# Attention and experts on one core: six small moves in the opening, the attention and the first slot

## The chip, the cores and the metric

The kernel runs on one NeuronCore of a Trainium2 chip. The metric is device time in microseconds (us), the median of three runs. Engines: TensorE (PE; its weight loads are PEld), VectorE (DVE), ScalarE (ACT), GpSimd (POOL) and SyncE (SP, which here issues DMAs). Each engine works through its own queue in order; semaphores tie the queues together.

## The reference

Three layers, one after the other. Attention: batch 4, 8 heads, 576 positions, head size 64, a causal window of 128 with a linear bias by distance:

```python
scores = scale * np.matmul(q, k.transpose(0, 1, 3, 2))
mask = (rel >= 0) & (rel < window)
scores = np.where(mask, scores + bias[None], -1000000000.0)
attn = np.exp(scores - scores.max(-1)); attn = attn / (attn.sum(-1) + 1e-09)
out = np.matmul(attn, v)
```

Its output (2304 tokens of 512) goes through a mixture of 8 experts of which each token uses one, `gate * (relu(x @ w1[e]) @ w2[e])` with the expert chosen by the largest gating logit, and then through a dense layer, `(relu(x @ w_in) ** 2) @ w_out` with 2048 inner columns.

## The kernel before

**Attention.** 40 units `(b, t, hh)`: a batch, a tile of 128 queries (t = 0 to 3; t = 4 is the half tile of 64), and one half of the heads. One loop over `k` (line 853) interleaves the units: in round k DVE takes the row maxima of unit k (`smax`, L272, for half tiles L274, after a predicated copy, L267 or L263), ACT its exponentials and their sums (`sexp`, L293, half tiles L295), TensorE the scores of unit k+1 (`sc`, L251, L253) and the transposes of unit k-2 (`tr`, L312), ACT and POOL bring these to SBUF under two masks (`ev`, L319 to L330), and TensorE multiplies with v (`pv`, L349, L356) for unit k-3. `norm` (L299 to L304) divides a half tile's exponentials by their sums, on DVE. There are two banks each of `s`, `t` and `v` in PSUM, and one each of `x` and `m`.

**Background.** Twice in a round, `background()` (line 828) lets every generator on a list do one step: `post` (L369 copy, L378 products with the gating weights, L393 or L391 evacuation, store of the rows to DRAM through SP at L395), `route(g0, G)` for 1 to 3 finished groups of 128 tokens (some fifteen small DVE steps; products L436, L437 and L465 in bank `m`; table update L468, L469), `first_slot` after the first eight groups (`CHECK`), which picks the expert of the first slot of 512 tokens, and `prefetch_first` (line 785), which gathers that slot's rows from DRAM (L674), loads its weights, splits them and turns the rows (`turn`: transposes L682, ACT cast L687, DVE remainder L689). The halves of a round are called half stages here.

**Weights.** Every float32 operand of an expert product is split in a rounded part and the remainder; a product then is three passes (`passes`, L694). `wsplit` splits a chunk of 128 x 1024: a cast (L604, on ACT, or on DVE if `quick`) and a subtraction (L605, on DVE, or on POOL for the eight chunks of the first slot). `up_first` (line 833) computes the first slot's up products as a generator that the last rounds of the attention begin; each of its eight f steps has three pieces of four products, with the relu of the step before (L718 ACT, L719 DVE) after the first piece and a split after every second step. `down_first` (line 901) does its down products. Four more slots follow, then the dense layer; both are long rows of products on TensorE.

**Opening.** Before the loop DVE builds the constants: `bias_consts` (L164), `near_bias` (L152, L170) and `tail_bias` (L152 and eight instructions at L185, into `biast`, which only half tiles read, in units of t = 4). SP issues the loads of five tiles of q, k and v.

The order of each queue is the order of the code: `kernel_scope = tc.manual_schedule()` leaves it as written.

Of the kernel before, what the change touches and what calls it, by code (L numbers as in the profile page):

```python
# [8 lines left out]
F32 = mybir.dt.float32  # L9
# [40 lines left out]
def attention_moe_kernel(ctx, tc, qh, kh, v, mid, wg, mb, w1, w2, win, wout, out):  # L50
# [130 lines left out]
    def tail_bias():  # L181
        wrap(relt, ownt)
        for h in range(H):
            r = slice(64 * (h % 2), 64 * (h % 2) + 64)
            dve.tensor_scalar(biast[r, h // 2, :], relt[r], slope(h), None, op0=ALU.mult)  # L185
# [94 lines left out]
    def sexp(u, i):  # L280
# [15 lines left out]
        if i:  # L296
            st[u] = ex.pop(u)

    def norm(u):  # L299
        r, e = rinv.pop(u), st[u]  # L300
        dve.tensor_scalar(r, r, 1e-9, None, op0=ALU.add)
        dve.reciprocal(r, r)
        for i in range(2):
            dve.tensor_scalar(e[:, i, 0, :], e[:, i, 0, :], r[:, i:i + 1], None, op0=ALU.mult)  # L304

    def tr(u):
        b, t, hh = u
# [94 lines left out]
    def route(g0, G):  # L402
# [24 lines left out]
        yield  # L427
        dve.tensor_reduce(mw, eq, axis=AX.X, op=ALU.max)
        dve.tensor_tensor(oh, eq, mw[:, :, None].to_broadcast(sh), op=ALU.is_equal)
        for i in range(G):  # L430
            aux.tensor_tensor(cum[:, g0 + i + 1, :], cum[:, g0 + i, :].bitcast(F32), ohf[:, i, :], op=ALU.add)
        yield
        if not last:
            yield
        rk_ = bank("m", (128, G, E))
        pe.matmul(rk_, upper, oh, start=True, stop=False)  # L436
# [21 lines left out]
        for i in range(G):  # L458
            dve.tensor_scalar(lh[:, 128 * i:128 * i + 128], iota, r[:, i:i + 1], val[:, i:i + 1], op0=ALU.is_equal, op1=ALU.mult)
        yield  # L460
        if not last:
            yield
        tp = bank("m", (128, E * NCH))
        for i in range(G):
# [136 lines left out]
    def wsplit(key, src=None, eng=None, sides=("left", "left"), quick=False):  # L601
        r = rawt.pop(key) if src is None else src
        h, l = wt(sides[0], F32R), wt(sides[1], F32R)
        (dve.tensor_copy if quick else act.copy)(h, r)  # L604
        (eng or dve).tensor_tensor(l, r, h.bitcast(F32), op=ALU.subtract)  # L605
        W[key] = h, l


# [64 lines left out]
        src = xd[:DUMP + SLOT, :] if s == 0 else xd[:, :]  # L673
        pool.indirect_dma_start(out=r[:], out_offset=None, in_=src, in_offset=bass.IndirectOffsetOnAxis(ap=gv[:, i:i + 1], axis=0))  # L674

    def turn(s, i, r, tag, n=512):
        if s not in xT:
            k = min(4, 1024 // n)
            xT[s] = [[wt("right", F32R)[:, :k * n].rearrange("p (c t) -> p c t", t=n) for _ in range(4 // k)] for _ in range(2)]
        p = bank(tag).rearrange("p (a b) -> p a b", a=4)  # L680
        for c in range(4):
            pe.transpose(p[:, c, :], r[:, 128 * c:128 * c + 128], ident)  # L682
        o = slice(128 * i, 128 * i + 128)
        xh, xl = xT[s]
        k = 4 // len(xh)
        for j in range(len(xh)):
            act.copy(xh[j][:, :, o], p[:, k * j:k * j + k, :])  # L687
        for j in range(len(xh)):
            dve.tensor_tensor(xl[j][:, :, o], p[:, k * j:k * j + k, :], xh[j][:, :, o].bitcast(F32), op=ALU.subtract)  # L689

    def passes(ps, pairs, first, last, **kw):
        n = len(pairs)
# [62 lines left out]
    def chunk_sides(s, j):  # L755
        return ("right", "right") if s == 0 and j < 4 else ("left", "left")
# [7 lines left out]
    def advance_split(upto):  # L764
        while pos[1] < min(upto, len(seq)):
            s, j = key = seq[pos[1]]
            wsplit(key, None, pool if s == 0 else None, chunk_sides(s, j), s == 0 and j < 3)
            pos[1] += 1

    convs = [(k_, i) for k_ in MOE_CHUNKS + DENSE_CHUNKS for i in range(2)]  # L770
# [14 lines left out]
    def prefetch_first():  # L785
        index(0, column(0))
        advance_load(1)
        yield
        for i in range(0, 4):
            gather(0, i)  # L790
            yield
        advance_load(2)
        yield
        advance_load(3)
        advance_split(1)
        for i in range(4):

            yield
            while not tail[0]:
                yield  # L800
            turn(0, i, xr[0][1][i], "v")
            if i % 2:
                advance_split(2 + i // 2)
        primed.append(True)
# [3 lines left out]
    LA = 5  # L808
    FIRST_UP = 40
    PIECES = 2  # L810

    kernel_scope = ctx.enter_context(tc.manual_schedule())
    bias_consts()
    pool.memset(spacer, 0.0)
    act.activation(spacer, spacer, AF.Exp)
# [5 lines left out]
    make_identity(nc, ident)  # L821
    tail_consts()
    route_consts()
    tail_bias()
    todo = []
    n = len(units)
    sc(units[0])
# [25 lines left out]
    for k in range(n + 3):  # L853
        now, last = k < n, 0 <= k - 2 < n
        if now:
            smax(units[k], 0)
            smax(units[k], 1)
            sexp(units[k], 0)
        if k + 1 < n:
            sc(units[k + 1])  # L860
        if last:
            tr(units[k - 2])
            ev(units[k - 2])
        if now:
            sexp(units[k], 1)
        background()
        if 0 <= k - 1 < n and units[k - 1][1] == 4:
            norm(units[k - 1])
        if k >= 3:
            pv(units[k - 3])  # L870
        tail[0] = k
        background()
        tail[0] = 0
        if k % 2 == 0:
            for ahead, load in ((5, load_qk), (4, load_v)):
                if k // 2 + ahead < len(tiles):
                    load(*tiles[k // 2 + ahead])
        for at, make in ((0, gate_weights), (2, route_loads), (5, logit_bias), (15, dump_rows)):
            if k == at:
                make()  # L880
        if k >= FIRST_UP and primed:
            for _ in range(PIECES):
                next(first, None)
                background()
# [365 lines left out]
```

## Time and profile before

| | us |
|---|---|
| median of three runs | 796.61 (794.02 to 796.89) |
| the profiled execution | 790.6 |
| its span, first to last instruction | 788.9 |
| TensorE busy | 755.2 |
| DVE / ACT / POOL busy | 402.8 / 301.0 / 258.3 |
| granted clock, mean of the span | 0.993 |

The span is one execution under the hardware profiler. Busy TensorE has modelled ends, since products are pipelined. The stages lie so: attention to about 143 us, the first slot's up products to about 175 us and its down products to 200 us, the other slots to about 372 us, the dense layer to the end. In a timeline row the bracket at the end tells how long the engine sat idle before the instruction and what ended that.

### The profile page before, as it was taken

How to read it: one execution, taken by the hardware profiler on the slowest of the kernel's cores; microseconds unless marked ns; L12 is line 12 of the kernel's file. 1: busy time of each engine (PE TensorE's matmuls, PEld its weight loads, DVE VectorE, ACT ScalarE, POOL GpSimd, SP SyncE). 2: the span in 40 equal slices, each digit the busy share in tenths (PEclk: the TensorE clock that was granted, in tenths of full speed). 3: DMA queues.
4: the chain of work that ended last, by engine and by line, in shares of the span. 5: the costliest groups of instructions: out<-in, count | busy, mean ns of one | idle time of the engine just before them, and what ended most of it. 6: DMA issues, size and time to landing. Idle time of an engine off the chain costs nothing.

```text
span 788.9 us, 12139 instructions
## 1 busy us (share of the span) xinstructions
PE 755.2 (96%) x4303; PEld 632.0 (80%) x4303; DVE 402.8 (51%) x1162; ACT 301.0 (38%) x763; POOL 258.3 (33%) x302
## 2 busy tenths in 40 slices
PE   6999896989999999998999999999999999999997
PEld 5777665777888888896898988888888888888995
DVE  7789887789997758785463522011310222011220
ACT  5675655335454444362452513021230413121230
POOL 4322354325453443523343603122040503122140
PEclk9999999999999999999899999999999999999999
DMA  8556440139756656461111200001000100001000
GB/s 269 171 177 205 154 169 27 55 127 377 257 174 200 214 186 214 147 214 55 42 54 54 81 28 27 1 15 66 28 1 0 54 27 27 0 13 42 27 1 27
DMA packets 39183, 79.00 MB, mean 100 GB/s; under 512 B 6608, under 2 KB 15056, under 8 KB 39120
## 3 DMA queue, kind: packets, MB, share of 16 engines
q1 hardware_dynamic: 36080, 68.23, 26.4%
q0 software_dynamic: 3040, 9.96, 3.4%
q8 instruction: 35, 0.57, 0.3%
q14 instruction: 28, 0.23, 0.1%
HBM read 62.19 MB, written 15.99 MB: 99 GB/s over the span
## 4 chain that ended last, share of the span: by engine, by line
PE 51%; issue 0%; DVE 0%; ACT 0%; POOL 0%; POOLq 0%; DVEq 0%
PE t L694 14%; PE s L694 13%; PE v L694 11%; PE x L694 6%; PE m L694 6%; PE m L682 0%; PE x L682 0%; DVE w L605 0%; ACT w L604 0%; DVE row L1115 0%; ACT w L1065 0%; DVE row L1084 0%; ACT row L1083 0%; DVE w L689 0%; ACT h L1077 0%
## 5 line engine op out<-in xcount | busy, mean ns | idle before, releaser
L694 PE MATMUL t<-w,h 128*128 128x512 f32 x888 | 208.7, 391 | 0.0
L694 PEld LDWEIGHTS t<-w,h 128*128 128x128 f32 x888 | 165.3, 188 | 33.8
L1078 POOL TENSOR_TENSOR h<-row,h 128x256 fp32r<-128x256 f32 (+1 forms) x96 | 100.5, 1051 | 271.5 <-ACT h L1077 264.9
L694 PE MATMUL s<-w 128*128 128x512 f32 (+2 forms) x888 | 175.8, 353 | 2.1 <-DVE h L719 1.7
L694 PEld LDWEIGHTS s<-w 128*128 128x128 f32 x888 | 146.9, 192 | 24.2 <-DVE h L719 2.6
L694 PE MATMUL v<-w,h 128*128 128x512 f32 x432 | 104.6, 393 | 0.0
L1084 DVE SCALAR_TENSOR_TENSOR row<-s,row 128x256 f32<-128x256 f32 (+1 forms) x50 | 27.6, 552 | 137.8 <-ACT row L1083 137.6
L694 PEld LDWEIGHTS v<-w,h 128*128 128x128 f32 x432 | 80.0, 188 | 16.3
L1083 ACT ACTIVATE row<-s 128x256 f32<-128x256 f32 (+1 forms) x50 | 24.3, 486 | 145.1 <-PE s L694 145.0
L694 PE MATMUL m<-w 128*128 128x512 f32 (+2 forms) x372 | 74.0, 348 | 0.0
L694 PE MATMUL x<-w 128*128 128x512 f32 (+2 forms) x372 | 74.0, 348 | 0.0
L694 PEld LDWEIGHTS m<-w 128*128 128x128 f32 x372 | 61.4, 189 | 8.4
L694 PEld LDWEIGHTS x<-w 128*128 128x128 f32 x372 | 61.4, 189 | 8.4
L293 ACT ACTIVATE e<-x,m 128x128 f32<-128x128 f32 x128 | 50.3, 395 | 40.3 <-DVE m L272 40.1
L605 DVE TENSOR_TENSOR w<-w 128x1024 fp32r<-128x1024 f32 x41 | 56.5, 1383 | 16.4 <-ACT w L604 16.2
L604 ACT CAST w<-w 128x1024 fp32r<-128x1024 f32 x46 | 48.0, 1049 | 7.6 <-DMA w<-w 4.8
L1077 ACT CAST h<-row 128x256 fp32r<-128x256 f32 (+1 forms) x96 | 48.6, 506 | 3.4 <-DVE row L1084 3.4
L640 POOL TENSOR_TENSOR w<-w,row 128x512 int32<-128x512 int32 x18 | 26.8, 1492 | 69.1 <-DVE row L639 39.2
L329 POOL TENSOR_SCALAR_AFFINE_SELECT pt<-pt 128x512 f32<-128x512 f32 (+1 forms) x32 | 19.2, 599 | 82.7 <-ACT pt L325 63.5
L251 PE MATMUL s<-kS,qS 64*128 64x256 f32 (+1 forms) x128 | 35.1, 401 | 7.2 <-DMA qS<-qh 3.8
L251 PE MATMUL t<-kS,qS 64*128 64x256 f32 (+1 forms) x128 | 35.1, 401 | 0.0
L349 PE MATMUL x<-pt,vS 128*64 128x128 f32 x448 | 32.4, 285 | 2.8 <-DVE ls L393 2.5
(247 smaller groups left out, 902.9 us busy)
## 6 DMA issues: line engine op xcount, KB each, us to landing
w<-w SPq DMA_DIRECT2D x40, 512.0 KB
w<-win SPq DMA_DIRECT2D x16, 512.0 KB
w<-wout SPq DMA_DIRECT2D x16, 512.0 KB
xd<-row SPq DMA_DIRECT2D x22, 256.0 KB
qS<-qh SPq DMA_DIRECT2D x19, 256.0 KB
row<-yd SPq DMA_DIRECT2D x18, 256.0 KB
vS<-vh SPq DMA_DIRECT2D x16, 256.0 KB
out_dram<-row SPq DMA_DIRECT2D x16, 256.0 KB
```

Of the source, the lines that this page charges most:

```text
L251: pe.matmul(s[j][:, i, c0:], qS[b, t][r, hp, :], kS[b][r, hp, 128 * t - 128 + c0:128 * t + 128], start=True, stop=True)
L293: act.activation(e[:, i, j, :], x[:, i, j, :], AF.Exp, bias=m[:, i, j:j + 1], scale=-1.0, accum_out=rinv[b, t][:, h:h + 1])
L329: pool.affine_select(out=diag, in_=prev[:diag.shape[0]], pattern=[[0, 2], [0, 2], [1, n]], channel_multiplier=-1, compare_op=ALU.is_ge, **kw)
L349: pe.matmul(W0[64 * j:64 * j + 64, hp, :], vS[b][:, k_, 64 * h:64 * h + 64], o[:, i, k_ - t + 1, j, :], start=n == 0, stop=n == len(kb) - ...
L604: (dve.tensor_copy if quick else act.copy)(h, r)
L605: (eng or dve).tensor_tensor(l, r, h.bitcast(F32), op=ALU.subtract)
L640: pool.tensor_tensor(a, a, r, op=ALU.add)
L694: pe.matmul(ps, l, r, start=first and i == 0, stop=last and i == n - 1, **kw)
L1077: act.copy(gh, gt)
L1078: pool.tensor_tensor(gl, gt, gh.bitcast(F32), op=ALU.subtract)
L1083: act.activation(r, p, AF.Relu)
L1084: dve.scalar_tensor_tensor(gt, p, 0.0, r, op0=ALU.max, op1=ALU.mult)
```

## The change

- `tail_bias()` leaves the opening; it is called at the end of round k = 1 instead.
- Ahead of everything TensorE makes six products of a zeroed 128 x 128 tile (cleared by DVE) into a PSUM bank that nobody reads.
- `norm` is parted: `norm_sums` (two small DVE instructions) comes right behind the round's `smax`; the two multiplications go from DVE to ACT and stand behind the round's second `sexp`, ahead of the first `background()`.
- In the route whose last group is the eighth (`g0 + G == CHECK`), two empty half stages are left out, one ahead of L436 and one ahead of L465.
- In `prefetch_first` the remainder of a turned tile (L689, DVE), and the weight split that follows every second tile, come one half stage after its transposes and casts.
- The subtraction of a weight split stays on POOL for chunks 0 to 2 of the first slot alone, there as two instructions of 512 columns; chunks 3 to 7 have it on DVE.

```diff
+    def norm_sums(u):
+        r = rinv[u]
+        dve.tensor_scalar(r, r, 1e-9, None, op0=ALU.add)
+        dve.reciprocal(r, r)
+
     def norm(u):
         r, e = rinv.pop(u), st[u]
-        dve.tensor_scalar(r, r, 1e-9, None, op0=ALU.add)
-        dve.reciprocal(r, r)
         for i in range(2):
-            dve.tensor_scalar(e[:, i, 0, :], e[:, i, 0, :], r[:, i:i + 1], None, op0=ALU.mult)
+            act.mul(e[:, i, 0, :], e[:, i, 0, :], r[:, i:i + 1])
...
         yield
-        if not last:
+        if not (last or g0 + G == CHECK):
             yield
         rk_ = bank("m", (128, G, E))
...
         yield
-        if not last:
+        if not (last or g0 + G == CHECK):
             yield
         tp = bank("m", (128, E * NCH))
...
-        (eng or dve).tensor_tensor(l, r, h.bitcast(F32), op=ALU.subtract)
+        n = 2 if eng is pool else 1
+        for i in range(n):
+            c = slice(1024 // n * i, 1024 // n * (i + 1))
+            (eng or dve).tensor_tensor(l[:, c], r[:, c], h[:, c].bitcast(F32), op=ALU.subtract)
...
-    def turn(s, i, r, tag, n=512):
+    def turn(s, i, r, tag, n=512, later=False):
...
-        for j in range(len(xh)):
-            dve.tensor_tensor(xl[j][:, :, o], p[:, k * j:k * j + k, :], xh[j][:, :, o].bitcast(F32), op=ALU.subtract)
+
+        def finish():
+            for j in range(len(xh)):
+                dve.tensor_tensor(xl[j][:, :, o], p[:, k * j:k * j + k, :], xh[j][:, :, o].bitcast(F32), op=ALU.subtract)
+
+        if later:
+            return finish
+        finish()
...
-            wsplit(key, None, pool if s == 0 else None, chunk_sides(s, j), s == 0 and j < 3)
+            wsplit(key, None, pool if s == 0 and j < 3 else None, chunk_sides(s, j), s == 0 and j < 3)
...
-            turn(0, i, xr[0][1][i], "v")
+            finish = turn(0, i, xr[0][1][i], "v", later=True)
+            yield
+            finish()
             if i % 2:
                 advance_split(2 + i // 2)
...
+    WARM = 6
 
     kernel_scope = ctx.enter_context(tc.manual_schedule())
+    warm = row()
+    dve.memset(warm[:, :128], 0.0)
+    idle = bank("m", (128, 128))
+    for i in range(WARM):
+        pe.matmul(idle, warm[:, :128], warm[:, :128], start=True, stop=True)
     bias_consts()
...
     route_consts()
-    tail_bias()
     todo = []
...
             smax(units[k], 1)
+        ended = 0 <= k - 1 < n and units[k - 1][1] == 4
+        if ended:
+            norm_sums(units[k - 1])
+        if now:
             sexp(units[k], 0)
...
             sexp(units[k], 1)
+        if ended:
+            norm(units[k - 1])
         background()
-        if 0 <= k - 1 < n and units[k - 1][1] == 4:
-            norm(units[k - 1])
...
-        for at, make in ((0, gate_weights), (2, route_loads), (5, logit_bias), (15, dump_rows)):
+        for at, make in ((0, gate_weights), (1, tail_bias), (2, route_loads), (5, logit_bias), (15, dump_rows)):
```

## Rows read from the trace of the kernel before

**Rows 1.** The page: busy us, share of the span, instructions.
```profile
PE 755.2 (96%) x4303; PEld 632.0 (80%) x4303; DVE 402.8 (51%) x1162; ACT 301.0 (38%) x763; POOL 258.3 (33%) x302
```

**Rows 2.** Windows: us, busy PE, PEld, DVE, ACT, POOL, granted clock, DMA, GB/s.
```profile
0.00:7.00 7.00, 2.34 (x16) 1.93 (x16) 4.44 (x22) 1.49 (x2) 5.71 (x31) 1.00 0.60 161
20.00:112.00 92.00, 85.54 (x836) 66.50 (x835) 79.58 (x447) 58.45 (x239) 31.29 (x52) 1.00 0.53 169
132.00:143.00 11.00, 7.71 (x64) 6.56 (x64) 9.64 (x43) 5.38 (x19) 6.62 (x8) 0.84 0.08 26
153.00:163.00 10.00, 7.34 (x37) 5.83 (x36) 9.07 (x33) 2.82 (x4) 2.55 (x2) 1.00 0.38 131
200.00:360.00 160.00, 160.00 (x751) 135.12 (x750) 127.85 (x192) 76.46 (x127) 68.49 (x70) 1.00 0.58 196
```

**Rows 3.** Timeline, opening and one later row: start us, us, instruction [idle before].
```profile
3.76 0.55 PE L251 MATMUL s<-kS,qS 64*128 64x128 f32 x1 [3.76 <-DMA qS<-qh]
5.68 0.42 PE L251 MATMUL t<-kS,qS 64*128 64x128 f32 x1
5.91 2.28 DVE L185 TENSOR_SCALAR biast<-relt 64x128 f32<-64x128 f32 x8
8.99 0.79 PE L251 MATMUL s<-kS,qS 64*128 64x256 f32 x1 [2.90 <-DVE m L272]
9.58 0.63 PE L251 MATMUL s<-kS,qS 64*128 64x256 f32 x1
11.10 0.43 DVE L267 COPY_PREDICATED s<-own,s 128x256 f32<-128x256 int32 x1 [1.11 <-PE s L251]
13.70 0.58 ACT L319 COPY pt<-v 128x512 f32<-128x512 f32 x1 [0.72 <-PE v L312]
13.91 0.38 PE L251 MATMUL s<-kS,qS 64*128 64x256 f32 x1
...
81.40 0.65 PE L312 MATMUL v<-ident,e 128*128 128x128 f32 x4
```

**Rows 4.** Groups by form: busy us, mean ns, idle before; then a wait, 20:112.
```profile
L304 DVE TENSOR_SCALAR e<-e,rt 128x128 f32<-128x128 f32 x16 | 4.6, 328 | 0.3
L295 ACT ACTIVATE e<-x,m 128x128 f32<-128x128 f32 x16 | 6.4, 402 | 9.1 <-DVE m L274 9.1
...
ACT e L293 <- DVE m L272: 27.5, 14, 4.0
```

**Rows 5.** Waits in 112:200: us in total, times, longest us.
```profile
DVE w L689 <- ACT w L687: 6.9, 4, 2.3
PE m L436 <- DVE ls L393: 2.3, 1, 2.3
```

**Rows 6.** Timeline around the route of the eighth group.
```profile
80.33 0.48 PE L251 MATMUL s<-kS,qS 64*128 64x256 f32 x1
81.72 0.32 DVE L469 TENSOR_TENSOR t_acc<-t_acc,m 128x160 f32<-128x160 f32 x1
...
99.02 0.97 PE L378 MATMUL m<-turned,row 128*128 128x144 f32 x6 [1.63 <-DVE r L487]
```

**Rows 7.** Groups of L605 by form, then timeline rows of the splits' stage.
```profile
L605 DVE TENSOR_TENSOR w<-w 128x1024 fp32r<-128x1024 f32 x41 | 56.5, 1383 | 16.4 <-ACT w L604 16.2
L605 POOL TENSOR_TENSOR w<-w 128x1024 fp32r<-128x1024 f32 x8 | 19.1, 2391 | 17.9 <-ACT w L604 7.8 <-DVE row L446 6.8 <-DVE w L604 3.3
...
71.22 0.66 DVE L449 TENSOR_TENSOR row<-row 128x480 fp32r<-128x480 f32 x1
153.91 2.75 DVE L449 TENSOR_TENSOR row<-row 128x480 fp32r<-128x480 f32 x1
159.17 1.19 PE L694 MATMUL s<-w 128*128 128x512 f32 x4 [1.68 <-DVE h L719]
161.81 1.05 ACT L604 CAST w<-w 128x1024 fp32r<-128x1024 f32 x1 [3.68 <-DMA w<-w]
162.97 2.54 DVE L449 TENSOR_TENSOR row<-row 128x160 fp32r<-128x160 f32 x1
```

## What the change does to the time: the prediction

> **What bounds the kernel now.** I read the page's busy shares first, then the windows by stage, then the waits of each engine inside the stages that the change touches. The page [rows 1] has TensorE busy for 96% of the span, but that is a mean over stages. The windows [rows 2] split it: from 200 to 360 us TensorE is busy for all 160.00 us, so there nothing but its own products sets the time, and an edit ahead of that stage is worth what it brings forward the moment at which that stage begins. Ahead of it lie the opening (to 15 us), the attention (to 143 us) and the first slot of experts (to 200 us). In 20:112 VectorE (DVE) is busy 79.58 of 92 us in 447 instructions with small gaps between them, and ScalarE (ACT) waits for its row maxima 27.5 us in 14 waits [rows 4]: DVE sets the pace of the attention, TensorE (85.54 us by modelled ends) is close behind, ACT and POOL have room. In 132:143 both TensorE and DVE lose time, and the granted clock falls to 0.84 [rows 2]. In 153:163 TensorE is idle 2.66 of 10 us.
>
> The sum is made against the profiled execution: span 788.9 us, 790.6 us with what lies around it. The median of the three runs is 796.6 us, 6.0 us above it; I take the sum's difference off that median.
>
> **The change part by part.**
>
> *Half tiles' constants behind the second group.* Today the eight `biast` instructions end at 5.91 + 2.28 = 8.19 us, and only then does DVE begin the row maxima of the first group; TensorE's third group of scores waits 2.90 us for the bank that these free, at 8.99 us [rows 3]. So one group's maxima take 0.8 us. Without the constants ahead of it DVE has done the first group before the second group's scores end, at 5.68 + 0.42 = 6.10 us, and the second by 6.9 us. There the constants come back: 2.28 us and the wrap, which I price as one of the eight (0.29 us), to 9.5 us. They are not removed, they only stand in a better place. The third group's scores also need tile 1 from memory: tiles 0 and 1 are 1.05 MB of q and k, and the window 0:7 moved 7 us x 161 GB/s = 1.13 MB [rows 2], so these products can't begin much before 7.4 us. They took from 8.99 to the 11.10 us at which DVE got them, 2.1 us, hence 9.5 us again. DVE's third group then starts at 9.5 instead of 11.10 us, 1.6 us earlier, and I take **1.5 us**. ACT follows it (at 13.70 us it waits only 0.72 us for its next transposes), so it carries. Bounds: 0 (the loads come later still) to 2.6 us (the constants' whole price).
>
> *Six unread products.* TensorE's first real product waits until 3.76 us for a load [rows 3]. At the opening its rows have half the speed of later ones (a 256-column product 0.63 us at 9.58, 0.38 us at 13.91), the lower of the two levels. Four products of their size take 0.65 us at 81.40 us, at the full clock, overlap and all, so six cost at most 2 x 6/4 x 0.65 = 2.0 us at the lower level, behind a DVE memset that has nothing ahead of it: they end before 3.76 us. I price them at 0 (bounds 0 to a loss of 0.3 us; that they gain is a rival). If that cover went, 2.0 us.
>
> *Half tiles scaled on ACT.* Sixteen DVE instructions of 0.29 us leave DVE (4.6 us [rows 4], of which twelve in 20:112, 3.4 us); the sums stay there, only earlier, behind maxima that need ACT's results of the group before. ACT gets sixteen instructions like its L295 row, 0.40 us each, 0.8 us per half-tile group, queued behind two exponentials and ahead of the copy at L369; the transposes of that group come one group later, so the room is there. DVE is the pace, but half of what it is freed of becomes waiting for TensorE: 4.6 x 0.45 = **2.0 us** (bounds 0 and 4.6).
>
> *First slot's split half a stage later.* The two halves of a POOL split cost POOL alone and are set at 0 (its L605 is read by products some stages later). DVE waits at L689 for ACT's cast four times, 6.9 us in all [rows 5], with the next group's maxima queued behind it although their scores are done. Now those maxima come first and the subtraction stands where its cast is long made. TensorE's own work in such a stage leaves little over half of the wait to be won: 6.9 x 0.5 = **3.5 us** (bounds 1 and 6.9). The last of these waits stands ahead of the 2.3 us for which TensorE waits for L393 [rows 5], after which the clock is granted at half: 0.16 x 11 us = 1.8 us of lost clock in 132:143 [rows 2]. If that idle time shortens, the drop may not come; I take **0.7 us** (0 to 1.8).
>
> *Two empty half stages fewer in the route of the eighth group.* The whole chain of the first slot (index, gathers, turns) comes one stage earlier; nothing reads it before stage 40, so that is worth 0 by itself. But its products now fall on half stages in which the single `m` bank is held: at 80.33 us TensorE goes on to the next scores today; with L436 ahead of them it waits until L469 has read the bank, 81.72 + 0.32 = 82.04 us [rows 6], 1.7 us. The later product (L465) puts a like wait at L378, which I set at half the first, 0.9 us; the 1.63 us of L378 behind L487 go away. Half of each reaches DVE, 0.5 x (1.7 + 0.9 - 1.6) = 0.5 us, and for the stages that these waits disturb behind them I take a **loss of 0.7 us** (bounds: loss 2.6, gain 1.6).
>
> *Splits of the first slot.* Five subtractions (chunks 3 to 7) go from POOL (2.39 us) to DVE (1.38 us), and the three others are cut in two on POOL. DVE's L449 takes 0.66 us at 71.22, but 2.75 us at 153.91 and 2.54 us at 162.97 (a third of the elements, some 0.3 us by itself), each time beside the L605 of POOL, ending with it [rows 7]. So POOL's two instructions cost DVE 2.1 + 2.2 us, and DVE gets 1.38 us each in exchange. The first frees 0.7 us ahead of the L719 for which TensorE waits 1.68 us, and lets the last group's rows go out 2 us sooner, and with them the load of chunk 4, queued behind that store on SP, whose cast waits 3.68 us. The second is about even: the moved instruction now waits for that cast, with the chain of the last route behind it. Chunks 5 to 7 meet a busy TensorE. **1.0 us** (bounds: loss 3.0, gain 2.66, the idle time of 153:163).
>
> The Trainium skill speaks against this part: its page "SBUF — State Buffer", section "Who interferes with whom", says that a VectorE instruction with two SBUF inputs and a GpSimd instruction that reads SBUF exclude each other, the later one blocked until the other ends. By that rule, which the three L449 rows bear out, the moved subtractions are themselves such instructions and would pay wherever POOL reads. POOL's 2.55 us in 153:163 are the split itself [rows 2], so nothing is left there to pay to, and the sum stays.
>
> Sum: 1.5 + 0 + 2.0 + 3.5 + 0.7 - 0.7 + 1.0 = **8.0 us**. 790.6 - 8.0 = 782.6 us for a profiled execution; 796.6 - 8.0 = **788.6 us** for the median.
>
> **The rivals.** (a) *Given back at the first slot.* TensorE reaches the first slot earlier and waits there for the route of the last group and the load behind it, as it does now in 153:163. Then only the splits' 1.0 us and a little of the rest count: 2 us, 794.6 us. For it: the 3.68 us wait for a load. Against: store, load and route hang on the same attention and move with it.
> (b) *DVE becomes the bound of the first slot: slower.* Each of the three splits of the up stage holds DVE for 1.38 us and up to 1.05 us for ACT's cast [rows 7], with the relu subtraction L719 behind it, and chunk 4 adds up to 3.68 us for its load: 3 x 2.43 + 3.68 = 11.0 us, less the 4.3 us of blocking that go. What the attention gained is swallowed by the same wait, and 6.7 us are left: 803.3 us. It decides from where L719 ends more than one f step (twelve products) after its own product, since there are two banks. For it: DVE is busy 9.07 of 10 us in 153:163. Against: 4.3 of these 9.07 us are the blocking.
> (c) *The six products raise the clock early.* The third and fourth groups' scores then take 1.05 instead of 2.1 us each; DVE stays bound by the constants until 9.5 us, but ACT's 0.72 us wait and some 0.7 us more go: 1.5 us more, 787.1 us. For it: TensorE would be busy from about 1 us on. Against: at most 2.0 us of products, then a pause until 3.76 us, and another from 6.10 us. If they do nothing, as I take it, that part of the change doesn't do what it is put there for. The Trainium skill ("TensorE: Matmul & The Clock Gate", section "Part 1: The HAM clock gate (the "warmup" mystery)") has the lower level as the default that activity lifts, which is this rival's rule; the rows at 9.58 and 13.91 us agree that it is lifted late.
>
> **How the numbers follow.** Forecast 0.56; (a) 0.22; (b) 0.12; (c) 0.10. A measurement of this kernel can tell about 0.5% (4 us) from no change, so faster by more is 0.56 + 0.10 = 0.66, within it 0.22, slower 0.12. The likeliest time is 788.6 us. Range: most terms at their better bounds give 13 to 14 us of gain, 783 us; upwards it takes in (a) and ends at 798 us, leaving out most of (b).
>
> **What would show it.** In the profile after: DVE's first maxima near 5 us and its third group near 9.6 us; the wait of L689 for L687 near zero; no L449 above 0.7 us, and L605 on POOL with 512 columns only; the rows of scores at 0.38 us from about the same time as now; a granted clock of 1.00 in the stretch that answers to 132:143; a first slot whose down products start some 8 us sooner, after which everything keeps its distance. It is wrong if TensorE's waits in the first slot grow, for L719 or for a load, or if the wait of L436 for L469 stretches each stage behind it.

## The result, and the profile after

The changed kernel takes 785.94 us (median of five executions, 784.64 to 788.06), the kernel before 796.43 us, 10.5 us more. The ratio on record is 0.9891, 95% interval 0.9871 to 0.9911, which is 8.7 us (7.1 to 10.3); the quotient of the two medians is 0.9868. Forecast were 788.6 us, 8.0 us less. The profiled executions tell less than that: 788.9 us of span before, 786.2 us after, 2.7 us apart. The profiled execution of before (790.6 us) is a quick one: of 56 later executions of that kernel, timed beside the experiments, two were quicker and the four medians lie between 793.6 and 795.6 us. That of the changed kernel (788.06 us) is the slowest of its five. So the traces show where steps moved, while sizes are taken from the timed ratios.

Windows of the kernel after, columns as in [rows 2], the same stretches:

```profile
20.00:112.00 92.00, 84.62 (x807) 65.30 (x803) 74.17 (x427) 58.72 (x238) 31.01 (x52) 0.96 0.52 169
132.00:143.00 11.00, 9.37 (x68) 7.47 (x69) 9.50 (x42) 5.33 (x17) 4.82 (x7) 0.69 0.20 58
153.00:163.00 10.00, 8.30 (x39) 6.45 (x38) 9.00 (x34) 2.84 (x4) 0.00 (x0) 1.00 0.56 185
```

In 20:112 DVE is busy 74.17 us instead of 79.58 us, and in 153:163 POOL has nothing left and TensorE 1.0 us more. But the granted clock is 0.96 in 20:112, where it was 1.00, and 0.69 in 132:143, where it was 0.84 and 1.00 was forecast. From 200 to 360 us TensorE is busy for all 160.00 us, as before.

Timeline of the kernel after, opening (start us, us, engine, instruction, idle time ahead of it):

```profile
1.17 2.93 PE L833 MATMUL m<-row 128*128 128x128 f32 x12 [1.17 <-DVE row L830]
4.03 0.58 PE L251 MATMUL s<-kS,qS 64*128 64x128 f32 x1
7.00 1.99 DVE L185 TENSOR_SCALAR biast<-relt 64x128 f32<-64x128 f32 x8
7.78 0.49 PE L251 MATMUL s<-kS,qS 64*128 64x256 f32 x1 [1.99 <-DMA qS<-qh]
8.06 0.63 PE L251 MATMUL s<-kS,qS 64*128 64x256 f32 x1
9.58 0.43 DVE L267 COPY_PREDICATED s<-own,s 128x256 f32<-128x256 int32 x1 [0.58 <-PE s L251]
```

The constants end at 8.99 us behind the second group's maxima, and DVE takes up its third group at 9.58 us, 1.52 us ahead of the 11.10 us of [rows 3] (9.5 us was forecast). In the last 0.58 us of that DVE waits for the scores, whose tile came late: of the two ways in which the forecast arrived at 9.5 us, the load's is the one that sets the time here. The six unread products stand in the trace as twelve records; they end at 4.10 us and hold the first real product back from 3.76 to 4.03 us. TensorE then waits 1.99 us for tile 1, and the third group's products take 0.63 us each, the lower level of the clock.

Waits of the kernel after in 112:200 (us in total, times, longest), answering to [rows 5], then timeline rows answering to [rows 6] and [rows 7]; old L449 is L453 here, L436 is L440, L469 is L473, L689 is L698, L719 is L732, L604 is L608:

```profile
DVE w L698 <- ACT w L694: 1.2, 3, 0.7
PE m L440 <- DVE ls L396: 1.9, 1, 1.9
```

```profile
79.49 0.28 PE L440 MATMUL m<-row,upper 128*128 128x16 f32 x1 [1.69 <-DVE t_acc L473]
80.40 0.63 PE L251 MATMUL s<-kS,qS 64*128 64x256 f32 x1
...
137.10 1.04 DVE L453 TENSOR_TENSOR row<-row 128x480 fp32r<-128x480 f32 x1
152.16 0.66 DVE L453 TENSOR_TENSOR row<-row 128x480 fp32r<-128x480 f32 x1
156.48 1.21 PE L707 MATMUL s<-w 128*128 128x512 f32 x4 [0.74 <-DVE h L732]
```

DVE's wait for ACT's cast went from 6.9 to 1.2 us. The wait of the route's product for the `m` bank is the 1.7 us that was forecast, but behind it the scores run at half speed (0.63 instead of 0.38 us), which no term held. The instruction beside the splits, which took 2.75 us, takes 0.66 us, and ACT's wait for the load went from 3.68 to 1.34 us (at 157.72 us). The same instruction takes 1.04 us at 137.10 us, where none above 0.7 us was forecast; no split runs there, but POOL's masks do (from 136.99 to 138.64 us).

### The profile page after: what moved, and what is told of

Read it like the earlier page. It is cut to its first block, busy times and chain, and to the rows that moved or that the text cites. A ratio compares the mean times of both kernels' runs of the same rounds, so it can differ in the third digit from the quotient of the medians.

```text
span 786.2 us, 12173 instructions
## 1 busy us (share of the span) xinstructions
PE 760.8 (97%) x4315; PEld 636.2 (81%) x4315; DVE 397.3 (51%) x1152; ACT 305.2 (39%) x779; POOL 247.2 (31%) x300
## 4 chain that ended last, share of the span: by engine, by line
PE 51%; DVE 0%; issue 0%; ACT 0%; POOL 0%; POOLq 0%; DVEq 0%
PE t L707 14%; PE s L707 13%; PE v L707 11%; PE x L707 6%; PE m L707 6%; PE m L689 0%; PE x L689 0%; DVE w L612 0%; ACT w L608 0%; DVE row L1139 0%; ACT w L1089 0%; DVE row L1108 0%; ACT row L1107 0%; DVE w L698 0%; ACT h L1101 0%
## 5 line engine op out<-in xcount | busy, mean ns | idle before, releaser
L612 DVE TENSOR_TENSOR w<-w 128x1024 fp32r<-128x1024 f32 x46 | 62.5, 1363 | 18.1 <-ACT w L608 17.9
L608 ACT CAST w<-w 128x1024 fp32r<-128x1024 f32 x46 | 48.0, 1048 | 4.3 <-DVE w L612 2.2
L1139 DVE TENSOR_SCALAR row<-t,gate 128x512 f32<-128x512 f32 x10 | 7.2, 751 | 52.2 <-PE t L707 52.2
```

The source lines that it names most:

```text
L612: (eng or dve).tensor_tensor(l[:, c], r[:, c], h[:, c].bitcast(F32), op=ALU.subtract)
L1139: dve.tensor_scalar(o, acc[j][i], gate2[:, g:g + 1], None, op0=ALU.mult)
```

## The experiments

Six kernels put one part of the change back each, the others combine parts or go further; line numbers of a run differ by up to three from those of the changed kernel. Differences between two ratios are turned into microseconds with 795 us; their interval is the root of the sum of the squares of the two half widths, some 0.003 or 2.4 us. The changed kernel stands in them with 0.9891. With the 0.9868 of its medians, each part put back would cost 1.8 us more than is said below, and the folded version would be level with the change; comparisons that leave the changed kernel out are not touched by this.

### The four smaller parts

*Constants* (`tail_bias()` ahead of the first group again):

```
+    tail_bias()
     todo = []
...
-    for at, make in ((0, gate_weights), (1, tail_bias), (2, route_loads),
+    for at, make in ((0, gate_weights), (2, route_loads),
```

> The changed kernel with the half tiles' constants made ahead of the first group again. Theory S: 1.5 us come back, ratio to the kernel before 0.991 (0.989 for the changed kernel); TensorE's third group of scores waits for the bank and DVE takes it up near 11.1 us instead of 9.6 us. Rival: the memory of the second tile of q and k sets the third group, ratio 0.989, DVE's third group within 0.3 us of 9.6 us.

Measured: 0.9921 (0.9897 to 0.9945), 2.4 us slower than the change. Its trace has the old opening again:

```profile
8.99 0.79 PE L251 MATMUL s<-kS,qS 64*128 64x256 f32 x1 [2.44 <-DVE m L272]
11.10 0.43 DVE L267 COPY_PREDICATED s<-own,s 128x256 f32<-128x256 int32 x1 [1.11 <-PE s L251]
```

The bank comes free at 8.99 us and DVE begins at 11.10 us, as in [rows 3], although the six products are there. The mechanism is shown; the interval holds the 1.5 us of theory S, and also, just, 0.

*Half tiles on DVE again:*

```
-            act.mul(e[:, i, 0, :], e[:, i, 0, :], r[:, i:i + 1])
+            dve.tensor_scalar(e[:, i, 0, :], e[:, i, 0, :], r[:, i:i + 1], None, op0=ALU.mult)
...
-        if ended:
-            norm_sums(units[k - 1])
...
+        background()
         if ended:
+            norm_sums(units[k - 1])
             norm(units[k - 1])
-        background()
```

(The sums go back behind the round's first background work with the products.)

> The changed kernel with the half tiles scaled on DVE again, sums and products together behind the background work. Theory S: 2.0 us come back, ratio 0.9915. Rival (the stages of the half tiles wait for TensorE and the split of the work on DVE and ACT makes little of it): the traces of the kernel before and after differ by only 0.5 us between 45 and 64 us, and there are four such places, of which two lie in stages with other waits: 0.5 to 1 us, ratio 0.990.

Measured: 0.9909 (0.9882 to 0.9935), 1.4 us slower. The interval doesn't separate the 2.0 us of theory S from its rival, nor from 0.

*Splits of the first slot on POOL again, each whole:*

```
-        n = 2 if eng is pool else 1
+        n = 1
...
-            wsplit(key, None, pool if s == 0 and j < 3 else None, ...
+            wsplit(key, None, pool if s == 0 else None, ...
```

> The changed kernel with all eight splits of the first slot on POOL, each whole. Theory S: 1.0 us comes back, ratio 0.990, and the tensor_tensor of the route that makes o2 (480 elements) takes 2.5 us or more beside a split of POOL. Rival (the turns now end earlier, so that the whole splits lie elsewhere): the time does not change, ratio 0.989. Second rival, by the run with the stages put back, where DVE's route instructions took 1.0 to 1.2 us beside POOL instead of 0.2 to 0.6 us and TensorE waited 3.5 us behind them: 3 us or more, ratio 0.993.

Measured: 0.9908 (0.9883 to 0.9934), 1.4 us slower; the second rival's 0.993 lies inside the interval by a hair. Timeline of this run:

```profile
129.95 3.01 DVE L435 TENSOR_TENSOR cum<-cum,row 128x8 fp32r<-128x8 f32 x3
134.19 0.25 PE L440 MATMUL m<-row,upper 128*128 128x24 f32 x1 [3.01 <-DVE ls L396]
152.91 2.49 POOL L612 TENSOR_TENSOR w<-w 128x1024 fp32r<-128x1024 f32 x1 [4.78 <-ACT w L608]
153.17 2.75 DVE L453 TENSOR_TENSOR row<-row 128x480 fp32r<-128x480 f32 x1
158.43 1.20 PE L707 MATMUL s<-w 128*128 128x512 f32 x4 [1.68 <-DVE h L732]
```

The 2.75 us beside POOL, TensorE's 1.68 us and a wait of ACT for a load (4.04 us) are all back; the second such row of [rows 7] (2.54 us) is not, it takes 0.33 us, and POOL's split begins behind it. From the first slot's first product to its first down product are 31.6 us here (143.06 to 174.69) and 30.9 us in the changed kernel (142.06 to 172.99): 0.7 us in the trace. The first two rows tell of another 1.1 us ahead of that, which the second rival's kind of wait costs: three small additions of the route's counts take 3.01 us beside a whole split (POOL, 130.60 to 132.93 us), 1.93 us beside a split in two halves in the changed kernel, and 0.57 us with no split beside them in the run with both steps back; TensorE then waits 3.01 instead of 1.94 us for L396. The Trainium skill ("SBUF — State Buffer", section "Who interferes with whom") has a VectorE instruction with two SBUF inputs contend with a GpSimd instruction that reads SBUF; by that rule the moved split frees the instruction at 153.17 us, and the trace agrees: 0.66 us without the split beside it, 2.75 us with it.

*No unread products:*

```
-    warm = row()
-    dve.memset(warm[:, :128], 0.0)
-    idle = bank("m", (128, 128))
-    for i in range(WARM):
-        pe.matmul(idle, warm[:, :128], warm[:, :128], start=True, stop=True)
```

> The changed kernel without the memset and the six unread products. Theory S: priced at 0, 785.9 us; the clock rises once, near 11.5 us, and the constants alone bring the third group of maxima to 9.6 us. Theory W (the products raise the clock at 4.65 us and this shortens the opening): the second group's scores are at half speed again, 0.4 us each product pair later, up to 0.5 us slower, 786.4 us. Against W: the first real product comes 0.27 us sooner without them (3.76 instead of 4.03 us), so 785.7 us is possible.

Measured: 0.9924 (0.9901 to 0.9947), 2.6 us slower: theory S (no effect) is not borne out, though its interval ends close to 0 (0.2 us), and the size is above what theory W allowed.

### The turns and the route: the two steps alone, together, and neither

*The turn's subtraction back in the half stage of its transposes:*

```
-            finish = turn(0, i, xr[0][1][i], "v", later=True)
-            yield
-            finish()
+            turn(0, i, xr[0][1][i], "v")
```

> The changed kernel with the subtraction of the first slot's turns in the same half stage as the transposes again. Theory S: 3.5 us for the waits of DVE for ACT's cast and 0.7 us of clock come back, 790.1 us; DVE waits at that subtraction about 7 us in four waits. Theory C: the turns lose 4.7 us again (what the trace shows between 123 and 130 us), but the half clock behind 134 us is 3.41 us long instead of 6.83 us, which gives 1.7 us back: 788.9 us.

Measured: 0.9972 (0.9954 to 0.9989), 6.4 us slower than the change, more than either theory. The waits are back in its trace (112:200, columns as in [rows 5]), while the clock of 132:143 is 1.00 there:

```profile
DVE w L698 <- ACT w L694: 7.2, 5, 1.9
```

*The route's two empty half stages back:*

```
-        assert g0 < CHECK or checked
...
-        if not (last or g0 + G == CHECK):
+        if not last:
             yield
```

(both places). With the long route the first slot's correction of the counts stands behind the next group's counts, as it does in the kernel before (there the counts are made from 98.0 us on and corrected at 103.7 us); the changed kernel asserts the other order, and the two runs with the long route leave the assertion out.

> The changed kernel with the two empty half stages put back into the route of the eighth group (the assertion on the order left out). Theory S (the terms of the prediction add up): the loss of 0.7 us goes, 785.2 us. Theory C (an idle wait of TensorE costs more than itself, because the granted clock falls behind it): the wait of L440 for L473 at 79.49 us (1.69 us) goes, and with it the two stretches of 3.41 us at half clock that begin at 79.74 and 103.63 us, 1.7 us each; that is up to 5 us, of which the first slot gets what the turns do not lose again: 782 to 783.5 us, and no half clock between 75 and 110 us.

Measured: 0.9943 (0.9923 to 0.9964), 4.1 us *slower*. Both theories had the wrong sign, and theory C's mark is missing too: the wait near 80 us went, but TensorE waits 2.24 us at 97.32 us instead, and the clock of 73:112 is 0.91, as in the changed kernel. The chain of the first slot must matter, so the other three of the four combinations were wanted. The shorter route alone, on the kernel before:

> The kernel before with the two empty half stages of the eighth group's route taken out, and nothing else. Theory S (the prediction): 0.7 us slower, ratio 1.001. Theory N (the first slot's chain is what decides at the end of the attention, where it meets the last route's instructions, and one stage earlier pays with or without the later subtraction): 2 to 4 us faster, ratio 0.995 to 0.9975. Theory D (it pays only together with the later subtraction, which makes the chain longer by four half stages): ratio 1.000 to 1.003, with TensorE's wait of 1.7 us for the route near 80 us and a half clock behind it.

Measured: 1.0066 (1.0048 to 1.0083), 5.2 us slower than before. Theory D's direction, with more than its price. The trace shows its wait, and a clock of 0.91 in 73:112, where it was 1.00:

```profile
82.38 0.38 PE L436 MATMUL m<-row,upper 128*128 128x16 f32 x1 [1.69 <-DVE t_acc L469]
```

```profile
73.00:112.00 39.00, 33.25 (x289) 25.48 (x290) 31.09 (x179) 20.56 (x84) 9.68 (x17) 0.91 0.39 124
```

The clock is not that of one execution alone: the mean over the six timed ones is 0.9845, against 0.9902 for the kernel before beside them. The difference, 0.0057 of 800 us, is at most 4.6 us of time, most of the loss.

Both steps back at once, the rest of the change kept:

> The changed kernel with both the route's two empty half stages and the early subtraction of the turns back; the rest of the change stays (the assertion on the order is left out). Theory S: the later subtraction with its clock is worth 4.2 us, the shorter route loses 0.7 us, so 3.5 us come back: ratio 0.9935. Theory I (the two steps pay only together: the shorter route alone costs what it cost on the kernel before, 5.2 us, and undoing it alone cost 4.1 us): from the run with only the turn put back, 0.9972 less 0.0066, that is 0.9906, so that both together are worth only about 1.2 us and the other edits some 7.5 us.

Measured: 0.9903 (0.9881 to 0.9925). That is theory I's number; theory S's 0.9935 lies outside. With the other edits in place the four combinations are:

| | subtraction at once | subtraction later |
|---|---|---|
| long route | 0.9903 | 0.9943 |
| short route | 0.9972 | 0.9891 |

Each step alone costs (3.2 and 5.5 us); both together are worth 1.0 us, give or take 2.4, that is, nothing that can be told from zero (2.8 us by the changed kernel's medians). The traces show where they collide. For each kernel: the scores of round k = 23 (the row near 73 us), the first slot's first product and its first down product (`t<-w,h`). Kernel before:

```profile
75.56 0.48 PE L251 MATMUL s<-kS,qS 64*128 64x256 f32 x1
143.81 0.50 PE L694 MATMUL s<-w 128*128 128x512 f32 x1
175.40 0.39 PE L694 MATMUL t<-w,h 128*128 128x512 f32 x1
```

Both steps back (last three rows: TensorE's wait near 97 us, the last of POOL's splits, and a DVE instruction of the late route that comes behind it, old L446):

```profile
72.67 0.48 PE L251 MATMUL s<-kS,qS 64*128 64x256 f32 x1
144.34 0.50 PE L706 MATMUL s<-w 128*128 128x512 f32 x1
175.25 0.39 PE L706 MATMUL t<-w,h 128*128 128x512 f32 x1
96.62 1.78 PE L381 MATMUL m<-turned,row 128*128 128x144 f32 x6 [2.23 <-DVE r L490]
134.50 2.50 POOL L611 TENSOR_TENSOR w<-w 128x512 fp32r<-128x512 f32 x2 [1.37 <-DVE w L607]
138.83 0.21 DVE L449 TENSOR_TENSOR row<-row 128x60 f32<-128x60 f32 x1
```

Long route, subtraction later:

```profile
73.37 0.48 PE L251 MATMUL s<-kS,qS 64*128 64x256 f32 x1
144.54 0.80 PE L706 MATMUL s<-w 128*128 128x512 f32 x1
177.10 0.39 PE L706 MATMUL t<-w,h 128*128 128x512 f32 x1
137.09 2.49 POOL L611 TENSOR_TENSOR w<-w 128x512 fp32r<-128x512 f32 x2
138.60 1.05 DVE L449 TENSOR_TENSOR row<-row 128x60 f32<-128x60 f32 x1
142.64 1.76 PE L352 MATMUL x<-pt,vS 128*64 128x128 f32 x14 [3.47 <-DVE ls L396]
```

Short route, subtraction at once:

```profile
72.37 0.48 PE L251 MATMUL s<-kS,qS 64*128 64x256 f32 x1
145.38 0.50 PE L707 MATMUL s<-w 128*128 128x512 f32 x1
177.90 0.39 PE L707 MATMUL t<-w,h 128*128 128x512 f32 x1
```

The changed kernel:

```profile
73.06 0.48 PE L251 MATMUL s<-kS,qS 64*128 64x256 f32 x1
142.06 0.50 PE L707 MATMUL s<-w 128*128 128x512 f32 x1
172.99 0.39 PE L707 MATMUL t<-w,h 128*128 128x512 f32 x1
```

From the scores to the first down product are 99.8 us before, 102.6 with both steps back, 103.7 and 105.5 with one of them (long and short route), 99.9 in the changed kernel. Each is one execution, and they are not alike in their sets: with both steps back it is the slowest of six (790.45 us, median 786.61), with the subtraction at once on the short route the second quickest of twelve. Still, the order of the last four is that of the timed ratios, and the changed kernel's lead of 3.8 and 5.6 us over the two single steps is near the timed 4.1 and 6.4. Counted to the first slot's first product the traces do not separate them so (71.7 us with both back, 71.2 and 73.0 with one): with the long route and the later subtraction the slower clock falls on the first slot's own products (0.80 instead of 0.50 us).

The later subtraction does not lengthen the chain by four half stages, as theory D has it. `turn` waits for the second half of a round in any case, so the transposes come one round apart with it and without it, from round 34 on with the long route and from round 33 on with the short one. What moves, by half a stage, is each subtraction and the split behind every second one. So without the shorter route the last split of POOL slips from 134.50 to 137.09 us, onto the late route's DVE instructions: one of them takes 1.05 instead of 0.21 us, three of them together 3.2 instead of 1.9 us, and TensorE waits 3.47 us for the DVE instruction queued behind them (L396). That collision is shown; that it accounts for all of the 3.2 us is not.

The shorter route puts the turns and their splits one round earlier, off these instructions, though beside the counts (1.93 instead of 0.57 us, above), and pays 1.69 us for the bank near 80 us. The slower clock behind that wait is not its price alone: in the traces of the two kernels with the long route TensorE waits 2.23 and 2.24 us near 97 us for another route instruction, and the clock of 73:112 is 0.91 there too. Without the later subtraction the short route has the 7.2 us of waits for ACT's cast.

### Versions that avoid the collision

*Folded:* the two empty half stages are put back and two others of the same route are taken out, so that the chain (and the correction of the counts) keeps its new place while the route's products fall on the old half stages:

```
-        if not (last or g0 + G == CHECK):
+        if not last:
             yield
...
         dve.scalar_tensor_tensor(r, cs, -128.0, rank, op0=ALU.mult, op1=ALU.add)
-        yield
+        if g0 + G != CHECK:
+            yield
         dve.scalar_tensor_tensor(val, js, 512.0, rank, op0=ALU.mult, op1=ALU.subtract)
         dve.tensor_tensor(val, val, idc[:, gs], op=ALU.add)
-        yield
+        if g0 + G != CHECK:
+            yield
```

(The first edit in both places.)

> The two empty half stages are put back, and two others of the same route are taken out instead (between js/r and val, and between val and lh), so that the first slot's chain keeps its new place but the two products on the m bank fall on the half stages of the kernel before. Theory S: as the run with the stages put back, 785.2 us. Theory C: 782 to 783.5 us, no wait of the route's products for L473 above 0.5 us near 80 us, no half clock between 75 and 110 us.

Measured: 0.9868 (0.9843 to 0.9893), 1.8 us faster than the change, which the interval doesn't separate from it. Its rows are what theory C asked for:

```profile
72.44 0.48 PE L251 MATMUL s<-kS,qS 64*128 64x256 f32 x1
78.88 0.28 PE L440 MATMUL m<-row,upper 128*128 128x16 f32 x1
137.43 0.50 PE L709 MATMUL s<-w 128*128 128x512 f32 x1
...
73.00:143.00 70.00, 61.00 (x568) 47.27 (x565) 61.56 (x315) 42.98 (x169) 31.68 (x44) 1.00 0.37 122
```

No wait for the bank, the clock at 1.00 throughout, and 65.0 us from the scores to the first slot, 4.0 us less than in the changed kernel. But this is the quickest of its five executions (780.33 us, median 783.73) beside the slowest of the changed kernel's, and the clock is not this route's doing alone: in the next run, with the same route, it is 0.96 in 73:112 and 0.71 in 132:143.

*Folded, without the unread products:*

> The folded version (two empty half stages put back, two others taken out) without the memset and the six unread products. With them its ratio was 0.9868. If the products are worth nothing: 0.987. If they are worth what the two runs of before differ by, 0.9924 against 0.9891, that is 2.6 us: 0.990. If they are worth what the openings show, 11.55 us for the second scores without them and 10.85 to 12.27 us with them: 0 to 0.7 us, 0.987 to 0.988.

Measured: 0.9916 (0.9894 to 0.9938), 3.8 us slower than the folded version. A second time the products are worth more than their effect in the opening.

*Folded, with eight more unread products behind the second group's scores:*

```
+        if k == 0:
+            for i in range(FILL):
+                pe.matmul(idle, warm[:, :128], warm[:, :128], start=True, stop=True)
```

> The folded version with eight more unread products behind the second group's scores, where TensorE waits 1.3 to 2.2 us for the second tile of q in the openings seen so far. Theory P (the pause lets the clock fall, or keeps it from rising, in some executions): TensorE's granted clock is full from about 6 us on in nearly each execution, the second stage's scores begin at 10.9 us as in the best openings; the profiled ones so far spread from 10.85 to 13.0 us with the first six products alone, so up to 1 us in the median and a smaller spread: ratio 0.9855 against 0.9868. Rival (the eight products stand in front of the real ones, or the second tile sets the opening anyway): 0.987 or worse.

Measured: 0.9851 (0.9829 to 0.9872): 1.4 us below the folded version, not resolved, and 3.2 us below the change, which its interval (2.3 us) does separate. By its ratio it is the fastest kernel of the study. The spread is no smaller than the folded version's (3.9 and 3.8 us). In its trace the filling covers the pause, and the real products behind it are at full speed:

```profile
5.86 2.05 PE L900 MATMUL m<-row 128*128 128x128 f32 x16
8.16 0.38 PE L251 MATMUL s<-kS,qS 64*128 64x256 f32 x1
```

*Folded, with the first slot's products one stage sooner* (`FIRST_UP = 39`):

> The folded version with the first slot's products beginning one stage sooner (FIRST_UP 39 instead of 40), two more pieces of four products beside the last stages. TensorE waits 1.94, 0.97 and 1.35 us there (129.5, 132.4 and 136.4 us in the folded version). Theory S (these products fill such waits): 1 to 2 us less, ratio 0.985. Rival (each stage is as long as DVE needs plus what TensorE has in front of it, and the products stand in front of the attention's own): no change or 1 us more, 0.987 to 0.988.

Measured: 0.9868 (0.9848 to 0.9887), no change, as the rival had it. From the scores to the first slot are 62.6 us (73.27 to 135.90) instead of 65.0 us, but to the first down product 97.3 us instead of 95.9 us: what is won at the start is lost later in that slot, where TensorE waits 2.12 us for the last route (0.96 us in the folded version) and the clock of 153:163 is 0.83:

```profile
157.53 0.38 PE L440 MATMUL m<-row,upper 128*128 128x8 f32 x1 [2.12 <-DVE t_acc L475]
```

## Why the prediction was right, and where it was not

The time lies in the range and the sign is right, but the sum came out by steps that erred in both directions: with both turn and route steps back the remaining four edits are worth 0.0097, 7.7 us (6.0 to 9.5), where their terms were 1.5 + 0 + 2.0 + 1.0 = 4.5 us; the turn and the route are worth 1.0 us, where their terms were 3.5 + 0.7 - 0.7 = 3.5 us. That these two errors nearly cancel is luck. Put back one by one the four cost 2.4 + 2.6 + 1.4 + 1.4 = 7.8 us, but two of them can't be told from 0 singly.

- **Constants, 1.5 us.** Right by mechanism and by the rows (9.58 us against the 9.5 us worked out, by way of the load); timed 2.4 us, with 1.5 us inside the interval.
- **Six unread products, 0.** The step that failed most. Their length was mis-sized (at most 2.0 us, measured 2.93 us, and the first real product 0.27 us later): the row it was taken from is four transposes with one record each, while six products leave twelve. So there was no pause ahead of the first real product either, and "priced at 0" took the pauses around them to undo any effect on the clock. Timed they are worth 2.6 and 3.8 us in two pairs. That is the direction of rival (c) and more than its 1.5 us; its mechanism, a third group at the upper level, stands in only three of the eight traces with the six products and the moved constants.
- **Half tiles on ACT, 2.0 us.** 1.4 us timed, 2.4 us either way: neither confirmed nor refuted. DVE's busy time in 20:112 fell by 5.4 us, of which the scaling accounts for 3.4 us by the forecast's count; with the scaling back on DVE it is 76.91 us, 2.7 us more than in the changed kernel.
- **Later subtraction, 3.5 us.** The wait did go (6.9 to 1.2 us), but the step read only that wait. It did not follow the splits behind the subtractions, of which the last, half a stage later, meets the late route; on the long route it costs 3.2 us, on the short one it is worth 6.4 us.
- **Clock in 132:143, 0.7 us.** Wrong: the clock there is lower than before, 0.69 against 0.84. TensorE still waits 1.9 us there for L396.
- **Route, a loss of 0.7 us.** The wait of 1.7 us came out to a hundredth. Two sentences beside it failed: that the chain's earlier place "is worth 0 by itself" as nothing reads it before stage 40, since POOL's split and DVE's route instructions do meet it before the end of the attention; and that half of each wait reaches DVE, since in the run on the kernel before the clock falls behind the wait. Without the later subtraction it costs 5.2 and 5.5 us in two pairs, with it it is worth 4.1 us.
- **Splits, 1.0 us.** Right in the rows it named in the splits' stage; the 1.04 us at 137.10 us stand beside POOL's masks, which it did not reckon with. That the two halves of a split "are set at 0" failed: they let DVE in between, and TensorE's wait for L396 is 1.1 us shorter than beside a whole split. So some 1.8 us in the trace, 1.4 us timed, not told from 0.

Of the rivals, (a) and (b) did not come: the waits of the first slot for L719 and for a load shrank. Everything keeps its distance behind the first down product, as forecast (613.5 us to the end before, 613.2 us after), but that product comes 2.4 us sooner in the profiled pair and not some 8 us; how much sooner it comes in the median execution the traces can't tell.

Two things stay open. The second stage's scores begin at 11.55 and 12.51 us in the two traces that lack the products (constants in their new place), and between 10.85 and 13.00 us in those that have them: the opening alone doesn't account for 2.6 and 3.8 us, and where the rest lies no trace shows. The mean granted clock of the timed executions, which doesn't count the opening up to the clock's first rise, is higher with the products in both pairs (0.9906 against 0.9895, folded 0.9938 against 0.9907, at most 0.9 and 2.4 us), so part of it may be slow stretches further on; that the products prevent them is not shown. And what the usual execution of the kernel before loses against the profiled one, 3 to 6 us, was not seen; its clock (0.991 in the mean of the 56, 0.993 in the profiled one) makes some 1.5 us of it at most.

## What to carry to other kernels

A step that moves work in a hand-laid order has to be followed to the last instruction of its chain, with the other engines that this chain then meets; two moves that each fix the other's damage are priced together. A wait of TensorE was followed by a slower clock in several of these stretches, though not in every trace, so a collision that is worth a microsecond by itself is worth a smaller rearrangement, as the folded route was. And where an early stage is short of load, a few unread products ahead of it and in its pauses can be tried for little.

## What the runs showed of the hardware

The same six products in front of the same scores did not do the same in each execution. Third group's products with the products ahead of them, folded version:

```profile
7.54 0.45 PE L251 MATMUL s<-kS,qS 64*128 64x256 f32 x1 [1.44 <-DMA qS<-qh]
7.84 0.38 PE L251 MATMUL s<-kS,qS 64*128 64x256 f32 x1
```

and in the run with both steps back, whose opening has the same instructions at the same times to 0.01 us:

```profile
7.54 0.76 PE L251 MATMUL s<-kS,qS 64*128 64x256 f32 x1 [1.43 <-DMA qS<-qh]
8.09 0.63 PE L251 MATMUL s<-kS,qS 64*128 64x256 f32 x1
```

The first is at the upper of the two levels (2.4 GHz) and the second at the lower (1.2 GHz), behind waits of 1.44 and 1.43 us, so the length of the wait doesn't tell them apart. In the changed kernel the level rose (0.27 us for a product of 128 columns at 4.75 us), fell again behind a wait of 1.99 us (0.63 us for 256 columns at 8.06 us) and rose a second time (0.38 us at 12.24 us). Of the eight traces with the six products and the moved constants three have the third group at the upper level; without the products it was the lower level in both traces. The Trainium skill ("TensorE: Matmul & The Clock Gate", section "Part 1: The HAM clock gate (the "warmup" mystery)") has the lower level as the default, released by activity, with a moment of release that varies from run to run. By that rule the products could shift the odds and no more; three of eight against none of two agree with it, but are too few to show it.

The same holds in the middle of the kernel. Ahead of the late route's product TensorE waits 1.94 us in the changed kernel, and the clock of 132:143 behind it is 0.69; in the folded version it waits as long, and the clock stays at 1.00 (73:143, shown above):

```profile
129.46 0.25 PE L440 MATMUL m<-row,upper 128*128 128x24 f32 x1 [1.94 <-DVE ls L396]
```
